# Loading q and k in 128 rows of 18 tokens and turning them with an output stride of 18, in a windowed-attention and expert-attention kernel

## The chip, the cores and the metric

The kernel runs on one core of a Trainium2 chip. Its engines work side by side, each through its own list of instructions in order: TensorE (PE in the profile, with its weight loads as PEld) multiplies matrices out of on-chip memory (SBUF) into the accumulators (PSUM); VectorE (DVE), ScalarE (ACT) and GpSimd (POOL) work on rows of elements; SyncE (SP) issues the transfers (DMAs) between the chip's large memory and SBUF, and ScalarE issues a few of them too. SBUF has 128 partitions, and an instruction of DVE works on all of them at once. The metric is the device time in microseconds of one execution, taken as the median of several runs.

## What is computed

Two steps follow each other. First, attention with a symmetric window of 32 tokens over 8 batches, 8 heads, 576 tokens and 64 elements per head; then, on the outcome, four small attention experts, of which two per token count.

```python
scores = scale * np.matmul(q, k.transpose(0, 1, 3, 2))
mask = np.abs(pos[:, None] - pos[None, :]) <= window
...
attn_out = np.matmul(attn, v).astype(np.float32)
x = attn_out.transpose(0, 2, 1, 3).reshape(B, S, H * D)
logits = x @ w_gate
...
for e in range(E):
    q = x @ wq[e]; k = x @ wk[e]; v = x @ wv[e]
    ...
    ye = a @ v @ wo[e]
```

All inputs and the output are 32-bit floats. q and k have the layout [batch, head, token, element], so that the 64 elements of a token lie together (256 bytes), and the tokens of a head follow each other.

## The kernel before

The product of q and k needs the elements of a head along the partitions, while they arrive with the tokens along the partitions. So each half of the heads of a batch (4 heads, called a group) is loaded with tokens along the partitions and then turned.

**Loading.** `load_qk` (line 268) fills one of three buffers per name, `qn0` to `qn2` and `kn0` to `kn2`, each of 128 partitions x 18 tokens x 64 elements. Head h of the group goes to partitions 32h to 32h+31. In the branch that the kernel before uses throughout, the tokens of a head are cut into 9 blocks of 64, and partition p of the 32 gets tokens 2p and 2p+1 of each block. The source is then made of pieces of two tokens, 512 bytes, and there is one transfer for each head: 32 partitions x 9 pieces, 144 KB. A load of one name for one group of one batch is four such transfers, 576 KB.

**Turning.** `turn` (line 288) makes two instructions of DVE (`STREAM_TRANSPOSE`, 128 x 576), one for each half of the 64 elements. Each turns squares of 32 x 32: element d of 32 tokens becomes partition d's run of 32 elements. Where they are written is set by the access pattern of the output, `T`. There the tokens lie in their natural order, and since the 32 tokens of one square are every second token, a square is written with a stride of two elements (8 bytes). The turned tiles `Tqn` and `Tkn` exist once for each group and half.

**The steps.** The order of all work is written out by hand in `ORDER`: each word is a step, and each engine meets its instructions in the order of the words. A step's name says what it does, with the batch and the group: `lq100` loads q of batch 1, group 0 (the third digit is the part, 0 for the whole), `lk` loads k, `lv` loads a part of v, `tq` and `tk` turn, `sc` multiplies q by k, `ex` takes exponentials (ACT), `mk` multiplies by the window's mask (DVE or POOL), `av` multiplies by v, `un` divides by the sums (DVE), `xt`, `xf` and `xb` turn and copy the outcome for the experts; `pp`, `ps`, `xe`, `se`, `po`, `oe` and the rest are the experts; `st` stores. A letter behind a colon picks a variant: for loads and turns `t` means the same layout through ScalarE's queue, `e` the other branch of the two functions. Batch 0 is loaded in two parts, so that work can begin on the first.

**What holds a load.** `load` (line 184) makes every transfer wait for the last TensorE instruction ahead of it in the list, so a load is not issued before its place in the list is reached. A load into a buffer also waits for the turns that read the buffer's former contents. And transfers of SP and ACT share eight semaphores in turn: each transfer waits until the one eight places ahead of it has landed. SP works through its list in order, so a transfer that waits holds all loads and stores behind it.

Of the kernel before, what the change touches and what calls it, by code (L numbers as in the profile page):

```python
# [24 lines left out]
NOE = 2  # L25

ORDER = """
    s_mask s_pads lq100 lk011:t tk011:t lk001:t tk001:t lq011 lq001 tq011 lq002 lk012:t lk002:t lq012 s_ones
    sc010@02 lv02 lk100 lv01 lv03 s_warm tq001 sc000@46 ex0101@2 ex0001@6 mk0001:g ex0000@4 lv00 s_ident mk0101:g
    tk002:t tk012:t tq002 sc001@24 ex0011@4 mk0011:g mk0000:g tq012 sc011@46 ex0111@6 tq100 tk100 mk0111:g lq110  # L30
    ex0100@0 ex0110@4 vc00:v ex0010@2 mk0010:v lk110 sc101@06 mk0110:v ex1011@6 tq110 ex1010@0 mk1010:v lv04 lw1
    sc100@24 vc01:g av02@0 tk110 lv13 ex1001@4 un02@0 mk0100:g av01@4 un01@4 av00@6 un00@6 lw0 ex1000@2 mk1000:v
    cw0:g av03@2 av04@0 mk1011:g un04@0 sc111@46 un03@2 ex1111@6 cw1:v xt02@0 lw2 cw2:g xt01@2 xf01:v@2 xb01:v
    lq200 lk200 xf02:a@0 xb02:v mk1001:g ex1110@4 xt00@6 xf00:a@6 sc110@04 ga0@6 gt0@6 xb00:a ex1101@4 lv10
    pp001@2 lv12 ex1100@0 mk1100:g lv11 lq210 pp000@0 pe000:v@0 pe001:a@2 pp010@2 pe010:v@2 mk1101:g mk1111:g
    ps003@0 ps000@4 xe003@0 se003 ps002@6 pv00@0 xe000@4 xe002@6 pp011@4 tq200 vc11:g ve00:a@0 pe011:a@4 ps001@6
    xe001@6 tk200 sc200@02 ex2001@2 ps013@4 lv14 xe013@4 mk1110:v lk210 vc10:v lk300 ps010@6 xe010@6 ex2000@0 ge0
    mk2000:g sc201@24 se000 ex2011@4 ex2010@2 se001 ps012@6 tq210 av12@0 mk2011:g un12@0 av10@4 mk2010:g lq300
    pv01@3 xe012@6 ve01:a@3 gm0 lk310 av13@6 av11@0 un10@4 un13@6 un11@0 se012 av14@4 un14@4 tk210 xt11@6 lw3
    xf11:a@6 lv23 xb11:g xt12@0 xf12:v@0 xb12:g xt10@4 lv22 mk2001:g xf10:v@4 xb10:v lv20 ps011@2 xe011@2 sc211@06  # L40
    ex2111@6 ex2110@0 mk2110:v se002 sc210@24 pp110@6 ex2100@2 mk2100:g ex2101@4 lv21 lq310 cw3:g pe110:a@6 gu0
    mk2101:g pp101@2 pe101:a@2 po00@6 pp100@2 tk300 lv24 oe00@6 pp111@4 se011 pt00@6 pe100:v@2 ps102@2 ps103@0
    pe111:a@4 xe102@2 xe103@0 tq300 ga1@7 gt1@7 lq400 ot00:a@6 mk2111:v sc301@24 ex3010@2 ex3011@4 ge1 tk310
    sc300@06 ex3001@6 ps100@2 xe100@2 lk400 tq310 vc21:g se010 av23@4 vc20:g av22@6 un23@4 ex3000@0 pv11@2 un22@6
    ve11:a@2 av20@0 un20@0 av24@7 lk410 un24@7 se013 ps111@4 xe111@4 mk3011:g ps101@2 lv31 xe101@2 av21@0 un21@0
    sc311@46 ex3110@4 tq400 lv30 sc310@02 ex3111@6 xt21@4 lq410 lv44 ex3100@0 mk3100:g ex3101@2 mk3101:g tk400
    xt20@0 xf21:v@4 xt22@2 po01@6 xf20:a@0 xf22:v@2 ps110@4 oe01@6 ps113@0 ga2@2 gt2@2 xb22:v xe113@0 lv33
    mk3110:v xe110@4 gm1 sc401@06 ex4011@6 mk3010:v tk410 lv32 tq410 ex4010@0 xb21:g sc400@24 mk3001:g lv34
    ex4000@2 mk4000:v lv41 ex4001@4 pv10@6 lv42 lq500 pt01@5 ot01:v@5 lv40 ve10:a@6 xb20:g pp200@3 pe200:a@3
    pp210@0 vc30:a pp201@6 gu1 pe210:a@0 pe201:v@6 pv20@4 ps203@6 lk500 ve20:v@4 ps112@0 mk3111:v xe203@6 xe112@0  # L50
    se100 gm2 ps200@2 xe200@2 mk3000:g lv43 vc31:g av31@6 pv21@5 ve21:v@5 un31@6 av30@0 mk4001:g av33@2 un30@0
    un33@2 mk4010:g lv53 se103 av32@4 un32@4 py02@0 ye02:a@0 av34@7 un34@7 lq510 py01@2 xt32@7 ye01:v@2 xf32:a@7
    xb32:v xt31@4 tk500 xf31:a@4 lk510 sc410@06 ex4100@0 sc411@24 ex4111@4 ex4101@6 py00@0 ex4110@2 vc41:g vc40:g
    se101 ye00:a@0 tq500 tq510 lv52 lv50 xt30@4 xf30:v@4 pp211@6 se102 po10@2 oe10@2 pe211:a@6 ps210@6 ps211@4
    ga3@0 gt3@0 lv54 xe210@6 xe211@4 sc500@26 ex5001@6 ex5000@2 se110 sc501@04 ex5011@4 mk4111:v ex5010@0 mk5001:v
    se112 se111 se113 po11@6 oe11@6 lk600 ps201@4 xb30:g mk4100:g lv51 mk4101:g ps212@2 xe201@4 xe212@2 av41@0
    un41@0 av40@6 ps213@4 xe213@4 mk4011:g un40@6 ge3 ps202@0 mk4110:g av44@2 lq600 tk510 se201 xe202@0 un44@2
    xb31:g pp300@4 pt10@0 pp310@6 se211 st02 pt11@1 ot11:a@1 tk600 mk5000:g vc50:g pp301@2 pe301:a@2 xt42@1
    pe310:v@6 pe300:v@4 av42@6 un42@6 av43@2 un43@2 xf42:v@1 st00 ot10:a@0 gm3 py12@0 se203 ye12:a@0 se213
    sc511@46 ex5110@4 ex5111@6 sc510@02 ge2 gu2 st01 lv62 py11@4 ex5100@0 mk5010:g vc51:g ex5101@2 lq700 ye11:a@4  # L60
    pp311@6 se200 pe311:a@6 lk610 xt41@2 gu3 xt40@4 xf40:v@4 lq610 xf41:a@2 pv30@6 mk5111:g ve30:a@6 mk5011:g
    se202 po20@4 xb42:a ps311@2 xe311@2 ps302@0 tq600 ga4@6 oe20@4 gt4@6 xe302@0 sc601@24 mk5100:g mk5110:g
    sc600@06 ex6010@2 ex6011@4 ex6001@6 ps301@2 xe301@2 ex6000@0 mk5101:v se210 se301 av51@4 lv71 xb40:g pv31@6
    ve31:a@6 lk710 gm4 un51@4 av54@7 un54@7 ps310@2 ps300@4 lk700 st12 ps312@0 av52@6 un52@6 xe310@2 av53@2
    xe300@4 un53@2 av50@4 lv61 un50@4 mk6010:v xe312@0 ps313@0 xe313@0 se302 ge4 ps303@2 py10@6 ye10:a@6 xt52@4
    xf52:v@4 xb52:v xe303@2 xt50@0 xf50:a@0 lv73 lv64 xt51@4 xb41:g xf51:a@4 xb51:a lq710 pp410@2 tk610 pe410:a@2
    mk6001:v tq610 pp411@0 pe411:a@0 se212 po21@4 pp401@2 st11 oe21@4 pe401:v@2 lv63 tk700 lv60 pt20@0 mk6000:v
    ot20:a@0 xb50:a se300 se303 po30@6 se312 vc61:g ps411@4 ps412@2 se311 pv40@0 xe411@4 oe30@6 xe412@2 pp400@4
    se412 pe400:v@4 ve40:a@0 tq700 sc610@26 sc611@04 ex6100@2 tk710 ex6101@6 mk6101:v ex6110@0 ps401@2 gu4 xe401@2
    ex6111@4 pp500@6 pp501@0 pe500:a@6 se313 se310 pt21@2 ot21:a@2 po31@4 ps402@6 xe402@6 pe501:v@0 oe31@4 tq710  # L70
# [559 lines left out]
```

## Time and profile before

| what | value |
|---|---|
| median of 3 runs | 264.48 us |
| lowest and highest run | 263.19 and 267.05 us |
| profiled execution, first to last instruction | 262.5 us |
| instructions | 11479 |
| read and written over the span | 152 GB/s |

The profile describes one execution with a span of 262.5 us; the median of the runs is 1.9 us above it. A page of the profile gives the busy time of each engine, then the chain of work that ended last, and then groups of instructions. In a row of a group stand the line, the engine, the operation, the tiles (output<-input), the shape, the count, the busy time in us and the mean of one in ns, and behind the second bar the idle time of the engine just ahead of them and what ended it. In a row of stretches of time stand from and to, the length, the busy time of each engine with the number of instructions in brackets, the granted TensorE clock as a share, the busy share of the 16 DMA engines, and GB/s.

### The profile page before, as it was taken

How to read it: one execution, taken by the hardware profiler on the slowest of the kernel's cores; microseconds unless marked ns; L12 is line 12 of the kernel's file. 1: busy time of each engine (PE TensorE's matmuls, PEld its weight loads, DVE VectorE, ACT ScalarE, POOL GpSimd, SP SyncE). 2: the span in 40 equal slices, each digit the busy share in tenths (PEclk: the TensorE clock that was granted, in tenths of full speed). 3: DMA queues.
4: the chain of work that ended last, by engine and by line, in shares of the span. 5: the costliest groups of instructions: out<-in, count | busy, mean ns of one | idle time of the engine just before them, and what ended most of it. 6: DMA issues, size and time to landing. Idle time of an engine off the chain costs nothing.

```text
span 262.5 us, 11479 instructions
## 1 busy us (share of the span) xinstructions
PE 228.9 (87%) x5013; PEld 183.2 (70%) x5024; DVE 193.2 (74%) x400; ACT 147.0 (56%) x221; POOL 127.2 (48%) x165
## 2 busy tenths in 40 slices
PE   0286999985989999699989999998899989999981
PEld 0165898664768888567878877886688758877650
DVE  2455896759899889998997956986876596667640
ACT  0223416761646557326745677776657657785852
POOL 5019706765686097337967906109734236322400
PEclk9995699999999999999999999999999999999997
DMA  8969989999974598886186798990021520124366
GB/s 166 209 171 180 228 160 211 204 198 226 199 177 138 161 209 176 170 196 162 34 205 201 157 162 159 216 290 15 2 63 42 186 80 2 32 92 157 126 216 208
DMA packets 89362, 40.60 MB, mean 155 GB/s; under 512 B 47072, under 2 KB 84960, under 8 KB 89312
## 3 DMA queue, kind: packets, MB, share of 16 engines
q1 hardware_dynamic: 86752, 38.69, 64.4%
q10 hardware_dynamic: 2560, 1.18, 2.4%
q8 instruction: 39, 0.64, 1.1%
q14 instruction: 11, 0.09, 0.1%
HBM read 30.42 MB, written 9.44 MB: 152 GB/s over the span
## 4 chain that ended last, share of the span: by engine, by line
PE 64%; DVE 16%; DMA 9%; issue 3%; ACT 3%; SPq 2%; POOL 1%; ACTq 0%; DVEq 0%
PE PS L179 57%; PE PS L182 7%; DVE A L340 5%; DMA qn<-in_q_dram 4%; DMA kn<-in_k_dram 4%; SPq L185 2%; ACT A L336 2%; DVE Tkn L298 1%; DVE RG L545 1%; DVE OE L546 1%; DMA out_dram<-Y 1%; DVE XN L368 1%; POOL V L173 1%; DVE Tqn L298 1%; DVE VE L173 1%
## 5 line engine op out<-in xcount | busy, mean ns | idle before, releaser
L179 PE MATMUL PS<-Tqn,Tkn 32*64 32x96 f32 (+5 forms) x2048 | 63.6, 307 | 16.9 <-DVE Tqn L298 11.6
L340 POOL TENSOR_TENSOR A<-A,MASKP 128x576 f32<-128x576 f32 x41 | 59.2, 1458 | 33.1 <-ACT A L336 32.5
L179 PEld LDWEIGHTS PS<-Tqn,Tkn 32*64 32x64 f32 (+1 forms) x2048 | 51.9, 158 | 29.4 <-DVE Tqn L298 12.0
L336 ACT ACTIVATE A<-PS 128x576 f32<-128x576 f32 x64 | 38.9, 650 | 41.0 <-PE PS L179 41.0
L506 ACT ACTIVATE ATE<-PS 128x1024 bf16<-128x1024 f32 x48 | 47.4, 1023 | 8.4 <-PE PS L179 6.8
L511 POOL TENSOR_SCALAR_AFFINE_SELECT ATE<-ATE 128x256 bf16<-128x256 bf16 (+1 forms) x80 | 31.4, 413 | 39.6 <-ACT ATE L506 24.2
L179 PE MATMUL PS<-V,A 128*64 128x65 f32 (+1 forms) x1280 | 39.6, 222 | 3.8 <-DVE XN L368 2.4
L179 PEld LDWEIGHTS PS<-V,A 128*64 128x64 f32 (+1 forms) x1280 | 36.1, 132 | 7.5 <-DVE XN L368 2.9
L173 POOL COPY V<-V 64x2048 f32<-64x2048 f32 (+1 forms) x12 | 21.8, 1820 | 27.3 <-DMA V<-in_v_dram 21.9
L298 DVE STREAM_TRANSPOSE Tkn<-kn 128x576 f32<-128x576 f32 (+2 forms) x36 | 23.2, 686 | 8.4 <-DMA kn<-in_k_dram 7.3
L298 DVE STREAM_TRANSPOSE Tqn<-qn 128x576 f32<-128x576 f32 (+2 forms) x36 | 23.2, 686 | 7.6 <-DMA qn<-in_q_dram 6.6
L340 DVE TENSOR_TENSOR A<-A,MASKP 128x576 f32<-128x576 f32 x23 | 25.3, 1109 | 3.0 <-ACT A L336 3.0
L368 DVE TENSOR_TENSOR XN<-PS,RC 128x512 f32<-128x512 f32 x32 | 22.1, 691 | 1.1
L179 PE MATMUL PS<-WV,XTB 128*128 128x256 bf16 (+1 forms) x192 | 18.8, 255 | 1.1 <-DVE OTT L173 0.8
L179 PE MATMUL PS<-WO,OTT 128*128 128x512 bf16 (+1 forms) x85 | 18.2, 341 | 1.4 <-ACT OTT L171 0.7
L179 PE MATMUL PS<-XTB,WK 128*128 128x288 bf16 x128 | 18.3, 286 | 1.0 <-DVE QKE L173 1.0
L182 PE MATMUL PS<-ident,XN 128*128 128x128 f32 x144 | 18.1, 275 | 1.1 <-DVE XN L373 0.9
L171 ACT COPY Y<-PS 128x1024 f32<-128x1024 f32 (+1 forms) x17 | 13.7, 826 | 9.3 <-PE PS L179 8.3
L179 PE MATMUL PS<-XTB,WQ 128*128 128x288 bf16 x128 | 18.1, 287 | 0.0
L179 PE MATMUL PS<-QKE 64*128 64x64 bf16 (+4 forms) x192 | 16.8, 277 | 1.4 <-DVE QKE L173 1.2
L182 PEld LDWEIGHTS PS<-ident,XN 128*128 128x128 f32 x144 | 15.8, 141 | 3.1 <-DVE XN L373 1.7
L179 PEld LDWEIGHTS <-ATE 128*128 128x128 bf16 x480 | 16.4, 97 | 2.2 <-POOL ATE L511 0.8
(71 smaller groups left out, 279.8 us busy)
## 6 DMA issues: line engine op xcount, KB each, us to landing
V<-in_v_dram SPq DMA_DIRECT2D x32, 256.0 KB, 4.7
out_dram<-Y SPq DMA_DIRECT2D x16, 512.0 KB, 3.8
qn<-in_q_dram SPq DMA_DIRECT2D x56, 144.0 KB, 4.3
kn<-in_k_dram SPq DMA_DIRECT2D x56, 144.0 KB, 4.3
V<-in_v_dram SPq DMA_DIRECT2D x8, 128.0 KB, 4.2
out_dram<-Y SPq DMA_DIRECT2D x16, 64.0 KB, 2.6
kn<-in_k_dram ACTq DMA_DIRECT2D x8, 80.0 KB, 3.5
qn<-in_q_dram SPq DMA_DIRECT2D x8, 80.0 KB, 2.8
```

The source lines that it names most:

```text
L171: nc.scalar.copy(o, i)
L173: eng(c).tensor_copy(o, i)
L179: last_pe[0] = nc.tensor.matmul(*a, **kw)
L182: last_pe[0] = nc.tensor.transpose(*a)
L185: r = q_.dma_start(o, i)
L298: nc.vector.transpose(T[:, 64 * m0:64 * m1].rearrange("q (m p o) -> q m o p", p=32, o=2), n_[:, 2 * m0:2 * m1, 32 * dh:32 * dh + 32].rearr ...
L336: nc.scalar.activation(AT[(2 * b + g) % NAT_][half][p], two(b0)[:, :, 0:HS], EXP, scale=scale_att)
L340: eng(c).tensor_tensor(out=ap, in0=ap, in1=MASK[:, None, HS * half:HS * half + HS].to_broadcast([128, 2, HS]), op=MULT)
L368: nc.vector.tensor_tensor(out=XN[T // 2][:, T % 2, :].rearrange("p (g h d) -> p g h d", g=2, h=4), in0=u[:, :, :, 0:64], in1=rc[:, :, :, N ...
L506: nc.scalar.activation(chunk(A, ch), two(b0), EXP, scale=scale_moe)
L511: nc.gpsimd.affine_select(ap, ap, pattern=[[0, n], [1, w]], compare_op=IS_GE, fill=0.0, base=0, channel_multiplier=-1)
L545: nc.vector.tensor_tensor(out=rg, in0=GG[b % 2][:, 2 * j:2 * j + 2, :], in1=rg, op=MULT)
```

## The change

The word of every load and turn of q and k of batches 1 to 7 in `ORDER` gets the letter `e`. Nothing else differs: the list has the same steps at the same places, the functions are the same, and batch 0 is loaded and turned as before.

```diff
-    s_mask s_pads lq100 lk011:t tk011:t lk001:t tk001:t lq011 lq001 tq011 lq002 lk012:t lk002:t lq012 s_ones
-    sc010@02 lv02 lk100 lv01 lv03 s_warm tq001 sc000@46 ex0101@2 ex0001@6 mk0001:g ex0000@4 lv00 s_ident mk0101:g
+    s_mask s_pads lq100:e lk011:t tk011:t lk001:t tk001:t lq011 lq001 tq011 lq002 lk012:t lk002:t lq012 s_ones
+    sc010@02 lv02 lk100:e lv01 lv03 s_warm tq001 sc000@46 ex0101@2 ex0001@6 mk0001:g ex0000@4 lv00 s_ident mk0101:g
...
-    se412 pe400:v@4 ve40:a@0 tq700 sc610@26 sc611@04 ex6100@2 tk710 ex6101@6 mk6101:v ex6110@0 ps401@2 gu4 xe401@2
+    se412 pe400:v@4 ve40:a@0 tq700:e sc610@26 sc611@04 ex6100@2 tk710:e ex6101@6 mk6101:v ex6110@0 ps401@2 gu4 xe401@2
```

With `e`, `load_qk` takes its first branch: partition p of a head's 32 gets the 18 tokens 18p to 18p+17, which lie together in the source, and the four heads follow each other, so that one transfer fills 128 partitions with one row of 4608 bytes each. `turn` takes its first branch too: the 32 tokens of a square are now 18 tokens apart, and the output is written with a stride of 18 elements (72 bytes) inside a square. The turned tiles hold the same elements at the same places as before.

| per load of q or k, batches 1 to 7 | before | after |
|---|---|---|
| transfers | 4 | 1 |
| partitions x pieces of one transfer | 32 x 9 of 512 bytes | 128 x 1 of 4608 bytes |
| bytes in all | 589,824 | 589,824 |
| turns (DVE) | 2, output stride 8 bytes | 2, output stride 72 bytes |

There are 28 such loads and 56 such turns. Each engine meets its instructions in the same order as before, and on SP 112 of the transfers become 28.

More of the change, by code (lines that the diff above doesn't have):

```diff
@@ L33 @@
-    cw0:g av03@2 av04@0 mk1011:g un04@0 sc111@46 un03@2 ex1111@6 cw1:v xt02@0 lw2 cw2:g xt01@2 xf01:v@2 xb01:v
[L34 to L37, printed above, removed]
@@ new lines @@
+    lq200:e lk200:e xf02:a@0 xb02:v mk1001:g ex1110@4 xt00@6 xf00:a@6 sc110@04 ga0@6 gt0@6 xb00:a ex1101@4 lv10
+    pp001@2 lv12 ex1100@0 mk1100:g lv11 lq210:e pp000@0 pe000:v@0 pe001:a@2 pp010@2 pe010:v@2 mk1101:g mk1111:g
+    ps003@0 ps000@4 xe003@0 se003 ps002@6 pv00@0 xe000@4 xe002@6 pp011@4 tq200:e vc11:g ve00:a@0 pe011:a@4 ps001@6
+    xe001@6 tk200:e sc200@02 ex2001@2 ps013@4 lv14 xe013@4 mk1110:v lk210:e vc10:v lk300:e ps010@6 xe010@6 ex2000@0 ge0
+    mk2000:g sc201@24 se000 ex2011@4 ex2010@2 se001 ps012@6 tq210:e av12@0 mk2011:g un12@0 av10@4 mk2010:g lq300:e
```

53 lines of the change are left out of this document (26 added, 27 removed).

## The prediction

> **What bounds the kernel now.** I read the busy times first, then the chain of work that ended last, then the stretches of time, because a share of the whole span mixes stretches with different limits.
>
> ```profile
> PE 228.9 (87%) x5013; PEld 183.2 (70%) x5024; DVE 193.2 (74%) x400; ACT 147.0 (56%) x221; POOL 127.2 (48%) x165
> ...
> PE 64%; DVE 16%; DMA 9%; issue 3%; ACT 3%; SPq 2%; POOL 1%; ACTq 0%; DVEq 0%
> ```
>
> TensorE sets the end, VectorE (DVE) is second on the chain, and transfers third. The stretches tell where each of them counts:
>
> ```profile
> 0.00:15.00 15.00, 3.23 (x68) 2.61 (x72) 5.62 (x27) 1.65 (x3) 3.87 (x12) 1.00 0.90 183
> 15.00:45.00 30.00, 26.94 (x672) 22.78 (x672) 22.71 (x41) 12.09 (x21) 15.41 (x14) 0.83 0.93 191
> 45.00:65.00 20.00, 15.80 (x361) 12.45 (x358) 14.10 (x22) 9.93 (x17) 14.03 (x14) 1.00 1.15 210
> 65.00:85.00 20.00, 18.74 (x470) 15.11 (x470) 18.49 (x34) 11.63 (x19) 14.10 (x15) 1.00 0.79 176
> 85.00:115.00 30.00, 27.82 (x678) 22.97 (x675) 27.04 (x55) 15.21 (x22) 13.31 (x11) 1.00 0.84 179
> 115.00:135.00 20.00, 18.80 (x497) 14.98 (x497) 17.52 (x29) 12.54 (x20) 16.33 (x19) 1.00 0.52 129
> 135.00:165.00 30.00, 29.76 (x668) 24.36 (x669) 22.75 (x54) 18.39 (x31) 16.49 (x22) 1.00 0.81 177
> 165.00:190.00 25.00, 23.33 (x504) 18.76 (x504) 20.53 (x38) 17.69 (x26) 12.13 (x15) 1.00 0.57 130
> ```
>
> The columns behind the length are PE, PEld, DVE, ACT and POOL, then the granted clock, the DMA share and GB/s. From 65 to 135 us DVE is nearly full: it idles 1.5 us of 20, 3.0 of 30 and 2.5 of 20. From 135 to 165 TensorE alone is full, and DVE has 7.2 us to spare. Up to 65 us the DMA engines are full. Whatever lengthens DVE is paid between 65 and 135, and whatever shortens transfers is won before 65.
>
> **The turns.** Their number does not change, only where they write. Today one whole turn takes
>
> ```profile
> L298 DVE STREAM_TRANSPOSE Tkn<-kn 128x576 f32<-128x576 f32 x28 | 20.0, 754 | 3.8 <-DMA kn<-in_k_dram 2.7 <-PE PS L179 1.1
> L298 DVE STREAM_TRANSPOSE Tqn<-qn 128x576 f32<-128x576 f32 x28 | 19.9, 752 | 2.3 <-DMA qn<-in_q_dram 1.2 <-PE PS L179 1.1
> ```
>
> and all 56 of them, 39.9 us of DVE, become turns with an output stride of 72 bytes. No turn of that kind is in the trace, so I look for pairs of DVE instructions of equal size, one writing its elements side by side, the other apart:
>
> ```profile
> L443 DVE TENSOR_TENSOR G<-NU,su x8: 194/266/1340, 71.8 to 247.0; 128x20 f32<-128x20 f32 x8
> L436 DVE TENSOR_TENSOR PK<-LT,m x8: 178/180/469, 61.9 to 235.3; 128x20 f32<-128x20 f32 x8
> L213 DVE MEMSET V<- x2: 112/112/112, 12.0 to 12.1; 128x64 f32 x2
> L220 DVE MEMSET QKE<- x3: 112/112/112, 1.2 to 1.3; 128x64 uint32 x3
> 1.17 0.26 DVE L220 MEMSET QKE<- 128x64 uint32 x3
> 12.00 0.23 DVE L213 MEMSET V<- 128x64 f32 x2
> ```
>
> The first pair: `G` is written through a rearranged pattern, each element 5 places (20 bytes) from the one before, `PK` side by side; both combine 20 elements with a broadcast. The minima, free of waiting, are 194 and 178 ns: 16 ns for 20 elements, 0.8 ns each. The second pair: line 213 writes the 64 ones of `V` 65 places (260 bytes) apart, line 220 writes runs of 32. Each instruction lasts 112 ns either way, which says no cost. But instructions overlap, and the spacing says otherwise: three of line 220 end 0.26 us after the first begins, so they start (0.26 - 0.112)/2 = 0.074 us apart; two of line 213 take 0.23, so they start 0.118 apart. That is 0.044 us more for 64 elements, 0.69 ns each. Over 576 elements the three readings are 0, 396 and 461 ns per turn; the upper end is a turn that doubles, +753 ns. No reason is seen why a wider stride should be a gain. I take 461 ns, because that row, like a turn, reads SBUF and writes it, while a memset reads nothing; and the spacing agrees. So 56 x 0.461 = 25.8 us more on DVE.
>
> The Trainium skill, page "Advanced Engine Details and Errata", section "Memory Cachelines", speaks against the change: SBUF has lines of 16 bytes, two accesses must fall in one line to cover its latency, and a new line at each access is penalised. At 8 bytes two elements share a line, at 72 none do. It gives no size of the penalty; `G` and the spacing agree with it, the duration of the memset does not. By it the sum would be the one below, and without it that of the first rival.
>
> What DVE pays in each stretch follows from the turns that lie in it:
>
> ```profile
> 15.00:45.00 30.00, 8.64 (x17) 0.83 0.93 191
> 45.00:65.00 20.00, 4.31 (x6) 1.00 1.15 210
> 65.00:85.00 20.00, 7.04 (x10) 1.00 0.79 176
> 85.00:115.00 30.00, 5.50 (x8) 1.00 0.84 179
> 115.00:135.00 20.00, 4.35 (x7) 1.00 0.52 129
> 135.00:165.00 30.00, 4.10 (x6) 1.00 0.81 177
> 165.00:190.00 25.00, 8.60 (x12) 1.00 0.57 130
> ```
>
> A longer DVE eats its own idle time first, but not all of it: part of that idle is time in which TensorE, itself late through DVE, has nothing ready. I let half of it absorb. From 65 to 85: 10 x 0.461 - 0.75 = 3.85. From 85 to 115: 3.7 - 1.5 = 2.2. From 115 to 135: 3.2 - 1.25 = 1.95. From 165 to 190: 5.5 - 2.2 = 3.3. From 135 to 165 the 2.8 us are covered by 7.2 of idle, and from 15 to 45 at most 17 turns, half of them of batch 0 and unchanged, by 7.3. Together 11.3 us; if all idle absorbs 5.5, if none does 17.0.
>
> **The loads.** Each of 28 loads becomes one transfer in place of four. Now:
>
> ```profile
> qn<-in_q_dram SPq DMA_DIRECT2D x56, 144.0 KB, 4.3
> ...
> L185 SPq DMA_DIRECT2D qn<-in_q_dram x72: 311/447/1551, 0.8 to 169.8; - x72
> ...
> SPq L185 <- DMA kn<-in_k_dram: 3.9, 5, 1.7
> ...
> 245.00:262.00 17.00, 11.06 (x140) 7.14 (x140) 6.41 (x17) 9.26 (x12) 2.06 (x6) 0.94 0.59 210
> ```
>
> SP saves 84 issues of 0.447 us, 37.5 us of its time; and since at most eight transfers are under way, a load takes one place of eight, not four. In the first 15 us, where nearly all pieces have 512 bytes, the engines moved 183 GB/s at a share of 0.90, or 203 when full; in the last 17, where stores with rows of 2 KB run, 210 at 0.59, or 356. A load of 589,824 bytes so takes 2.9 us of full engines now and, if long rows of a load run like those of a store, 1.7 after: between 0 and 1.2 us less each.
>
> The Trainium skill, page "DMA: Bandwidth & Descriptors", section "Rules for kernel authors", asks for 128 partitions and large single transfers. By it alone the change would be won; the rows say where that can count.
>
> At most places it can't: a load is held until its place in the list, and its turn has slack. It counts at the start, where the chain is four waits for transfers in a row, and from 49 to 57 us, where DVE stands still for loads:
>
> ```profile
> 1.26 3.93 DMA kn<-in_k_dram
> 5.57 2.95 DMA kn<-in_k_dram
> 8.54 2.75 DMA kn<-in_k_dram
> 11.30 2.85 DMA qn<-in_q_dram
> ...
> 49.91 1.44 DVE L298 STREAM_TRANSPOSE Tkn<-kn 128x576 f32<-128x576 f32 x2 [1.19 <-DMA kn<-in_k_dram]
> 54.26 1.22 DVE L173 COPY V<-V 64x1536 f32<-64x1536 f32 x1 [2.27 <-DMA V<-in_v_dram]
> 56.71 1.44 DVE L298 STREAM_TRANSPOSE Tqn<-qn 128x576 f32<-128x576 f32 x2 [1.23 <-DMA qn<-in_q_dram]
> ```
>
> The start: `lq100` is the very first load on SP and shares the engines with batch 0. It gives back up to 1.2 us; I take 1.0. From 45 to 65 the three stalls are 4.7 us, while TensorE idles 4.2. Loads issued earlier take the stalls away; six longer turns put 2.8 back. I take 1.5 us won. What is late next there is DVE itself.
>
> **The sum** against the profiled execution: 262.5 + 11.3 - 1.0 - 1.5 = 271.3 us, and with the 1.9 us by which the median of the runs lies above that span, 273.2. With all idle absorbed 267.4, with none 278.9.
>
> **The rivals.** *The wide stride costs nothing* (the memset's 112 ns are the truth). Then only the loads count: 1.0 at the start and, of the 4.2 us that TensorE idles from 45 to 65, about 3; the rest waits for other things. 262.5 - 4.0 + 1.9 = 260.4 us, between 257.5 and 263. It decides while a turn gains less than about 240 ns: at that price the same rule gives 1.65 + 0.4 + 0.45 + 0.7 = 3.2 us of loss, as much as the loads then win (1.0 and 2.2). Against it stand `G` and the spacing, for it that turns drain at their own pace.
>
> *A turn doubles*, +753 ns. By the same rule: 6.75 + 4.5 + 4.0 + 6.8 = 22.1 us, the stretch from 45 to 65 wins nothing, the start 1.0: 262.5 + 21.1 + 1.9 = 285.5 us. For it speaks only that no row has a stride inside squares of 32.
>
> *The start gets worse*: the one transfer of `lq100` holds its place of the eight until all 576 KB have landed, and the transfer of k that comes eight later waits for it, ahead of batch 0's first scores. If the chain's second link, 2.95 us, starts 1.2 later, the 1.0 won is 1.2 lost: 275.4.
>
> That the change does not do what it says is excluded for the instructions, which are as described in the compiled program; whether one transfer of 128 rows keeps all 16 engines busy no row shows.
>
> **How the numbers follow.** Costly stride as summed 0.62, costless 0.25, doubling 0.08, worse start 0.05. The forecast is the first, 273. Its own range is 266 to 280. For 8 in 10 the range also has to reach most of the costless case: 259 to 281; outside stay the doubling, the lower third of the costless case and a little of the first, about 0.19. Two per cent, about what separates a change of this kernel from none, is 5.3 us: faster means under 259.2, slower over 269.8. Faster: a third of the costless case, 0.08. Slower: 0.7 of the first and both last, 0.56. Within: the rest, 0.36.
>
> **What would show it.** The row of the turns: near 1210 ns (right), near 750 (first rival), near 1500 (second). DVE's busy time: 219 us. The stretch that holds batch 1 to 4's turns after 65 us: DVE with hardly any idle, TensorE waiting for turned tiles. The first scores: at 13.8 us in place of 14.80. The three stalls from 49 to 57 gone. The prediction is wrong if turns are slow and yet hidden (the time within 265), or if loads win over 6 us.

## The result: 281.0 us, slower than forecast, and the profile after

| | before | changed |
|---|---|---|
| median of the runs | 265.43 us | 281.0 us |
| lowest and highest run | 263.19 and 267.05 | 279.47 and 284.89 |
| ratio, with its interval | | 1.0652 [1.0577, 1.0727] |
| ratio in a second comparison, 5 rounds | | 1.0643 [1.0592, 1.0694] |

The forecast was 273 us with a range up to 281. The direction was right and the loss was nearly twice the size: 15.6 us where 8.7 had been summed. Ratios here and below compare the fast executions of both kernels alone (an execution more than 1.5 per cent above the fastest of its kernel counts as slow), so they are not the quotients of the medians, which go by all. All rows of the changed kernel below are from the profile of the second comparison (span 281.0 us, 18.5 above that of before; the medians of that comparison, 283.53 and 266.12 us, are 17.4 apart). First its page:

```profile
PE 233.5 (83%) x5024; PEld 185.0 (66%) x5024; DVE 219.3 (78%) x400; ACT 147.2 (52%) x221; POOL 125.6 (45%) x165
...
PE 53%; DVE 32%; DMA 6%; issue 5%; ACT 2%; ACTq 0%; DVEq 0%
...
L294 DVE STREAM_TRANSPOSE Tqn<-qn 128x576 f32<-128x576 f32 x28 | 32.3, 1237 | 3.0 <-PE PS L179 3.0
L294 DVE STREAM_TRANSPOSE Tkn<-kn 128x576 f32<-128x576 f32 x28 | 32.5, 1240 | 0.5 <-PE PS L179 0.5
L340 DVE TENSOR_TENSOR A<-A,MASKP 128x576 f32<-128x576 f32 x23 | 31.9, 1397 | 2.6 <-ACT A L336 2.6
```

A turn takes 1237 to 1240 ns where it took 752 to 754: 485 more, and 461 had been forecast. DVE's busy time is 219.3 us, as forecast to the microsecond (217.0 and 217.5 in two other executions), and its share of the chain doubled from 16 to 32 per cent. But the last row is a surprise, and makes the agreement partly luck: DVE's 23 products with the window's mask, which the change does not touch, took 25.3 us before,

```profile
L340 DVE TENSOR_TENSOR A<-A,MASKP 128x576 f32<-128x576 f32 x23 | 25.3, 1109 | 3.0 <-ACT A L336 3.0
```

and take 31.9 now; some other rows of DVE got shorter. The stretches of the prediction again, with the columns as there:

```profile
15.00:45.00 30.00, 23.30 (x658) 19.58 (x647) 26.19 (x37) 10.30 (x18) 14.64 (x13) 0.94 0.71 171
45.00:65.00 20.00, 16.81 (x367) 13.11 (x364) 17.18 (x22) 11.89 (x20) 14.27 (x14) 1.00 0.77 241
65.00:85.00 20.00, 17.03 (x389) 13.35 (x396) 18.72 (x32) 9.06 (x15) 12.23 (x14) 1.00 0.62 157
85.00:115.00 30.00, 24.76 (x616) 20.43 (x600) 27.20 (x40) 15.31 (x24) 14.64 (x12) 1.00 0.57 152
115.00:135.00 20.00, 18.68 (x402) 14.65 (x405) 18.43 (x36) 9.12 (x15) 6.93 (x11) 0.91 0.54 143
135.00:165.00 30.00, 27.08 (x640) 21.94 (x630) 27.10 (x46) 16.17 (x27) 21.76 (x22) 1.00 0.52 161
190.00:215.00 25.00, 20.74 (x507) 17.05 (x497) 19.67 (x32) 12.54 (x21) 11.11 (x16) 0.86 0.08 18
```

The DMA engines are no longer full ahead of 65 us (0.71 and 0.77 of their time, before 0.93 and 1.15), and the granted clock is below 1.00 in two stretches behind 100 us where before it was not. Where the 18.5 us arise is read from TensorE's list, which is the same in both kernels: the start of the same product in the two traces, taken next to the forecast's boundaries.

| stretch (us, before) | delay of TensorE at its end | gained in it | forecast |
|---|---|---|---|
| 0 to first score product | 0.9 | 0.9 | -1.0 |
| to 45 | 2.8 | 1.9 | 0 |
| 45 to 65 | 1.9 | -0.9 | -1.5 |
| 65 to 85 | 4.2 | 2.3 | 3.85 |
| 85 to 115 | 9.2 | 5.0 | 2.2 |
| 115 to 135 | 10.4 | 1.2 | 1.95 |
| 135 to 165 | 12.2 | 1.8 | 0 |
| 165 to 190 | 18.05 | 5.85 | 3.3 |
| 190 to the end | 18.5 | 0.45 | 0 |

Two stretches stand out, 85 to 115 and 165 to 190, and with them the start and the stretch to 45. The last is worse than the table says, for there the two traces also differ in the clock: before has it at 0.50 from 21.0 to 31.2 us, this execution of the changed kernel only from 31.3 to 34.7. So TensorE was 0.8 us early at 25 us and 2.7 early at 31.6, and lost 5.5 from there to 45. The timeline of the changed kernel (start, length, engine, line, operation, and in brackets the idle time ahead of it and what ended it) shows what TensorE waited for there:

```profile
12.54 6.16 PE L179 MATMUL PS<-Tqn,Tkn 32*128 32x192 f32 x132 [12.54 <-DVE Tqn L298]
...
31.80 4.83 PE L179 MATMUL PS<-V,A 128*64 128x65 f32 x112 [1.16 <-DVE A L340]
37.61 0.67 PE L179 MATMUL PS<-V,A 128*32 128x65 f32 x32 [0.99 <-DVE XN L368]
...
65.17 0.67 PE L179 MATMUL PS<-V,A 128*32 128x65 f32 x32 [1.93 <-DVE XN L368]
...
96.67 0.70 PE L179 MATMUL PS<-Tqn,Tkn 32*64 32x160 f32 x26 [1.10 <-issue]
...
115.22 1.03 PE L179 MATMUL PS<-WV,XTB 128*128 128x256 bf16 x8 [3.66 <-DVE OTT L173]
...
193.42 1.41 POOL L340 TENSOR_TENSOR A<-A,MASKP 128x576 f32<-128x576 f32 x1
193.94 4.60 DVE L340 TENSOR_TENSOR A<-A,MASKP 128x576 f32<-128x576 f32 x1
195.17 2.75 POOL L340 TENSOR_TENSOR A<-A,MASKP 128x576 f32<-128x576 f32 x2
199.19 0.75 DVE L173 CAST QKE<-PS 128x576 bf16<-128x576 f32 x1
199.99 5.75 PE L179 MATMUL PS<-Tqn,Tkn 32*128 32x128 f32 x128 [4.01 <-DVE QKE L173]
```

In before these two waits are 0.82 us and none, and the product that DVE starts at 193.94 reads

```profile
179.62 0.72 DVE L340 TENSOR_TENSOR A<-A,MASKP 128x576 f32<-128x576 f32 x1
```

The wait of 3.66 us at 115 is in part as forecast: two turns (109.73 to 114.21) stand ahead of the copy of `OTT` in DVE's list, 2 x 2 x 0.485 = 1.9 us longer together. Ahead of them, a product with the mask at 107.35 takes 2.45 us where it took 0.75, beside a copy of POOL. The wait at 200 is not as forecast. One product of DVE lasts 4.60 us in place of 0.72; it ends at 198.54, which is 0.62 us behind the end of POOL's three products (195.17 + 2.75 = 197.92). It did not work for 4.60 us, it stood until POOL was through and then took its own time. And the 128 score products behind the wait last 5.75 us. Three windows of the same trace, laid on the places where the clock falls, show one reason:

```profile
31.30:34.70 3.40, 2.90 (x54) 2.91 (x56) 3.40 (x5) 0.00 (x0) 0.00 (x0) 0.50 0.45 85
116.70:120.10 3.40, 3.40 (x54) 2.72 (x56) 2.29 (x7) 2.22 (x3) 0.00 (x0) 0.50 0.61 174
198.60:205.40 6.80, 5.41 (x122) 4.52 (x124) 5.20 (x11) 1.19 (x2) 0.00 (x0) 0.50 0.01 2
```

At each of them the granted clock is 0.50, for 3.4 or 6.8 us, behind or within a wait of TensorE. So there are at least three things to separate: DVE's lost time itself, what waits do to the clock, and what the shift does to DVE and POOL, which meet at other times.

### The profile page after: what moved, and what is told of

Same layout as the page of the kernel before. It is cut to its first block, busy times and chain, and to the rows that moved or that the text cites. A ratio compares the mean times of both kernels' runs of the same rounds, so it can differ in the third digit from the quotient of the medians.

```text
span 283.1 us, 11352 instructions
## 1 busy us (share of the span) xinstructions
PE 237.3 (84%) x5013; PEld 189.1 (67%) x5024; DVE 217.5 (77%) x400; ACT 147.3 (52%) x221; POOL 125.7 (44%) x165
## 4 chain that ended last, share of the span: by engine, by line
PE 53%; DVE 31%; DMA 6%; issue 6%; ACT 2%; ACTq 0%; DVEq 0%
PE PS L179 47%; DVE A L340 7%; PE PS L182 7%; DVE Tqn L294 5%; DVE Tkn L294 5%; DMA kn<-in_k_dram 4%; DVE XN L368 2%; DVE OE L546 2%; DVE QKE L173 2%; ACT A L336 1%; DMA qn<-in_q_dram 1%; DMA out_dram<-Y 1%; DVE RG L545 1%; DVE L L424 1%; DVE XTB L173 1%
## 5 line engine op out<-in xcount | busy, mean ns | idle before, releaser
L179 PE MATMUL PS<-Tqn,Tkn 32*64 32x160 f32 (+5 forms) x2048 | 65.6, 310 | 23.0 <-DVE Tqn L298 12.3
L179 PEld LDWEIGHTS PS<-Tqn,Tkn 32*64 32x64 f32 (+1 forms) x2048 | 52.8, 159 | 36.4 <-DVE Tqn L298 12.3
L179 PE MATMUL PS<-V,A 128*64 128x65 f32 (+1 forms) x1280 | 41.6, 228 | 7.9 <-DVE XN L368 4.3
L179 PEld LDWEIGHTS PS<-V,A 128*64 128x64 f32 (+1 forms) x1280 | 37.7, 137 | 12.3 <-DVE XN L368 4.8
L294 DVE STREAM_TRANSPOSE Tqn<-qn 128x576 f32<-128x576 f32 x28 | 32.3, 1236 | 2.8 <-PE PS L179 2.8
L294 DVE STREAM_TRANSPOSE Tkn<-kn 128x576 f32<-128x576 f32 x28 | 32.5, 1239 | 0.5 <-PE PS L179 0.5
L173 POOL COPY V<-V 64x2048 f32<-64x2048 f32 (+1 forms) x12 | 21.4, 1783 | 22.8 <-DMA V<-in_v_dram 12.2
L340 DVE TENSOR_TENSOR A<-A,MASKP 128x576 f32<-128x576 f32 x23 | 28.7, 1258 | 2.6 <-ACT A L336 2.6
L182 PE MATMUL PS<-ident,XN 128*128 128x128 f32 x144 | 20.6, 302 | 0.4 <-DVE XN L373 0.2
L182 PEld LDWEIGHTS PS<-ident,XN 128*128 128x128 f32 x144 | 18.4, 157 | 2.5 <-DVE XN L373 0.9
L171 ACT COPY Y<-PS 128x1024 f32<-128x1024 f32 (+1 forms) x17 | 13.6, 826 | 11.9 <-PE PS L179 8.0
L179 PEld LDWEIGHTS <-XTB 128*128 128x128 bf16 (+1 forms) x192 | 14.9, 106 | 6.6 <-issue 4.7
```

Source lines behind the costliest of these rows:

```text
L171: nc.scalar.copy(o, i)
L173: eng(c).tensor_copy(o, i)
L179: last_pe[0] = nc.tensor.matmul(*a, **kw)
L182: last_pe[0] = nc.tensor.transpose(*a)
L294: nc.vector.transpose(T[:, :].rearrange("q (p o) -> q o p", o=18)[:, o0:o1], n_[:, o0:o1, 32 * dh:32 * dh + 32])
L340: eng(c).tensor_tensor(out=ap, in0=ap, in1=MASK[:, None, HS * half:HS * half + HS].to_broadcast([128, 2, HS]), op=MULT)
```

## The experiments

### The change once more

> The changed kernel once more, for a profile beside the others. Theory A (turns cost 485 ns more each, and the stalls they make let the granted TensorE clock fall to half, which lengthens matmuls in turn): 278 to 283 us, turns at 1.24 us each, TensorE busy 7 to 9 us more than before for the same matmuls, and some 15 us more at half clock. Theory B (the larger transfers cost a good part of the loss, by holding their places among the eight in flight): the same time, but the engines wait for transfers of q and k by 4 us or more over the parts behind the start.

Measured: 283.04 us (277.96 to 283.66). And with five rounds:

> The changed kernel again, beside the next two on one chip. Both theories: 1.055 to 1.07 of the kernel before.

Measured: 283.53 us, ratio 1.0643 [1.0592, 1.0694], the profile shown above. In the trace of the first of these two runs the clock was at half for 24 us ahead of 250 us, in the second for 13.7, and yet the spans are 281.5 and 281.0 us: where it falls, and how often, differs between executions of one kernel, and the sum of the time at half does not tell how long one takes. What stays in both is the waits ahead of the products at 115 and 200 us (2.23 and 3.98; 3.66 and 4.01). The first is 1.4 us shorter where the product with the mask ahead of the turns takes 0.75 us (in the other, 2.45). Theory B's waits are not there: DVE waits for q and k at the start alone (8.7 us, batch 0), and no longer behind it.

### The two halves apart

One kernel has the old loads and the new turns, the other the new loads and the old turns. In both the tokens then stand in another order, with the same instructions and sizes, so that only their times can be used.

```diff
-    lq200:e lk200:e ... tq200:e ... tk200:e
+    lq200 lk200 ... tq200:e ... tk200:e        (turns_only, all of batches 1 to 7)
+    lq200:e lk200:e ... tq200 ... tk200        (loads_only)
```

> The loads are those of the kernel before (four transfers of 512-byte pieces), the turns write with the stride of 18; the tokens so come out in another order, with the same instructions and sizes. Theory A: all of the loss and the loads' gain gone as well, 280 to 286 us. Theory B: the turns alone give what was summed for them, 262.5 + 11.3 and 1.9 on top, some 275 us or less.

Measured: 278.93 us, ratio 1.0507 [1.0392, 1.0621], between the two theories. Again with five rounds:

> The wide turns with the old loads (tokens in another order), once more. If the loads add a loss of their own when turns are slow: 1.045 to 1.055 of the kernel before, at least 0.8 per cent below the changed kernel. If they add nothing: within 0.6 per cent of the changed kernel.

Measured: 1.0479 [1.0405, 1.0553].

> The loads are single transfers of 128 rows, the turns write with the stride of 2 as before; again the tokens come out in another order. Theory A: faster than before, 258 to 262 us, with the three stalls of VectorE between 49 and 57 us gone. Theory B: slower than before, 267 us or more.

Measured: 265.91 us, ratio 1.0018 [0.9969, 1.0067]: neither theory. In its trace TensorE is 0.8 us late at the first product and 1.3 late at 45 us, then 1.3 early at 65, and it stays 1.1 to 1.4 early from there on. So the loads win 2.6 us between 45 and 65, where the forecast had 1.5, and lose 1.3 ahead of it, where the forecast had a gain of 1.0. The whole loss is the turns', and the loads add to it only beside slow turns: 1.0643 against 1.0479.

### The price of a stride

A kernel of DVE instructions alone, each three times on 576 elements per partition; the rest of the computation is left out.

```python
for _ in range(3): nc.vector.transpose(wide(k), P1)   # L79 to L85: output stride k = 1, 2, 3, 4, 5, 8, 18
for _ in range(3): nc.vector.transpose(W1[:, 0:576].rearrange("q (p o) -> q o p", o=18), P1)   # L90
for _ in range(3): nc.vector.tensor_tensor(out=flat(k), in0=W2[:, 0:576], in1=W2[:, 576:1152], op=MULT)   # L91 to L97
for _ in range(3): nc.vector.tensor_tensor(out=W2[:, 0:576], in0=flat(k), in1=W2[:, 576:1152], op=MULT)   # L98 to L104
```

> Leaves out the whole computation: only instructions of VectorE on 128 x 576 32-bit elements, three of each kind, turns and products of two tiles, with an output stride of 1, 2, 3, 4, 5, 8 and 18 elements, and products with such a stride on an input. If what counts is how many elements share 16 bytes: turns near 735 ns at 1 and 2, between at 3, near 1235 from 4 on, all alike, and the same steps for products. If it is a collision of certain strides: 8 and 18 differ from 4 and 5 and from each other. If it is the turn's own drain: products keep their time at all strides.

Measured, in groups by line (the last number ahead of the second bar is the mean in ns):

```profile
L90 DVE STREAM_TRANSPOSE W<-src 128x576 f32<-128x576 f32 x3 | 3.8, 1258 | 0.1
L85 DVE STREAM_TRANSPOSE W<-src 128x576 f32<-128x576 f32 x3 | 3.8, 1257 | 0.1
L97 DVE TENSOR_TENSOR W<-W 128x576 f32<-128x576 f32 x3 | 3.7, 1235 | 0.1
L104 DVE TENSOR_TENSOR W<-W,W 128x576 f32<-128x576 f32 x3 | 3.7, 1229 | 0.1
...
L82 DVE STREAM_TRANSPOSE W<-src 128x576 f32<-128x576 f32 x3 | 3.6, 1199 | 0.1
...
L81 DVE STREAM_TRANSPOSE W<-src 128x576 f32<-128x576 f32 x3 | 2.8, 938 | 0.1
...
L80 DVE STREAM_TRANSPOSE W<-src 128x576 f32<-128x576 f32 x3 | 2.3, 779 | 0.1
...
L79 DVE STREAM_TRANSPOSE W<-src 128x576 f32<-128x576 f32 x3 | 2.3, 759 | 0.1
```

A turn takes 759, 779, 938 and 1199 ns at strides of 4, 8, 12 and 16 bytes, and 1257 at 72. The step is at 16 bytes: up to 8 a stride costs nearly nothing, at 12 some 160 to 180 ns, from 16 on 420 to 500 ns on 576 elements, 0.72 to 0.87 ns each. A product pays the same whether it writes (1235) or reads (1229) with the stride. This is the rule of the Trainium skill that the prediction weighed ("Advanced Engine Details and Errata", "Memory Cachelines": lines of 16 bytes, two accesses in one line, a penalty else), and this trace agrees with it and gives the size that the page does not have.

### DVE's lost time, or something else that the stride disturbs

Old loads, old turns, and behind each whole turn a second one of 416 elements into a tile that nobody reads:

```diff
                 nc.vector.transpose(T[:, 64 * m0:64 * m1].rearrange(...), n_[...].rearrange(...))
+                if b > 0:
+                    nc.vector.transpose(PAD[:, :].rearrange("q (o p) -> q o p", p=32), n_[:, 0:13, 32 * dh:32 * dh + 32])
```

> The kernel before, with an extra turn of 13 squares (416 elements, about 490 ns) into a spare tile behind each of the 56 whole turns; all writes side by side or 8 bytes apart. Theory A (the loss is the time that VectorE loses, wherever it comes from): slower than before by as much as the wide turns alone, 1.04 to 1.06. Rival (wide writes also hinder other engines' access to SBUF): clearly less, under 1.03.

Measured: 280.76 us, ratio 1.0462 [1.04, 1.0525], as with the wide turns alone (1.0479). An added turn lasts 569 ns, so that DVE's list got 31.9 us longer, by wide turns 27.2. Filling it with work of no use, at no wide stride, costs much the same: the stride acts through DVE's time.

### The first load

```diff
-    s_mask s_pads lq100:e ... tq100:e
+    s_mask s_pads lq100 ... tq100
```

> The changed kernel with the very first load (q of batch 1, group 0) and its turn as in the kernel before. If that single transfer of 576 KB, ahead of batch 0's, is what delays the start: the first products begin at 11.6 to 11.9 us in place of 12.3 to 12.6, and the time falls by about 1 us. If not: the first products begin as late as with the change.

Measured: 281.34 us, ratio 1.0603 [1.0552, 1.0655]; the first score product starts at 11.61 us, before at 11.64, in the change at 12.54. The ratio is not clear of the change's 1.0643, but the trace shows that the loss at the start is that one transfer's. In the change's chain, k's first transfer takes longer to land, and the second starts 1.1 us later than in before (5.57):

```profile
1.25 5.39 DMA kn<-in_k_dram
6.66 2.97 DMA kn<-in_k_dram
```

### Steps moved away from the waits

In the change, and as a control in the kernel before, the steps that stood on DVE ahead of three awaited results are put behind them:

```diff
-    pv01@3 xe012@6 ve01:a@3 gm0 lk310:e ... un14@4 tk210:e
+    pv01@3 xe012@6 ve01:a@3 lk310:e ... un14@4 gm0 tk210:e
-    mk3010:v tk410:e lv32 tq410:e ex4010@0 ... pe201:v@6 pv20@4
+    mk3010:v lv32 ex4010@0 ... pe201:v@6 tk410:e tq410:e pv20@4
-    ex6101@6 mk6101:v ex6110@0 ... pe501:v@0 oe31@4
+    ex6101@6 ex6110@0 ... pe501:v@0 mk6101:v oe31@4
```

> The changed kernel with four VectorE steps at later places of the list: gm0 behind un14, tk410 and tq410 behind pe201, the mask product mk6101 behind pe501. Theory A (a slow turn costs where it, or a step it pushes into GpSimd's work, stands ahead of something TensorE needs): the waits ahead of av14, pv20 and sc701 (1.8, 2.2 and 4.0 us) shrink to under 1 us each and the time falls by 5 to 9 us. Rival (VectorE is full there, so another wait takes their place): less than 2 us.

Measured: 283.84 us, ratio 1.0665 [1.0602, 1.0728].

> The kernel before with the same four steps moved. Theory A: the wait ahead of av14 (2.4 us) shrinks, the rest had little wait: 1 to 3 us faster than before. Rival: no difference, or slower.

Measured: 265.48 us, ratio 0.9988 [0.995, 1.0026]. Nothing was won. Two turns behind the copy of `OTT` made the next awaited result late instead, by 3.6 us, and behind the moved mask product this came up in the timeline of the changed kernel with moved steps:

```profile
200.45 3.71 DVE L440 TENSOR_TENSOR NU<-EX,PK 128x20 f32<-128x20 f32 x1
...
201.35 2.76 POOL L340 TENSOR_TENSOR A<-A,MASKP 128x576 f32<-128x576 f32 x2
...
205.52 4.85 PE L179 MATMUL PS<-Tqn,Tkn 32*128 32x128 f32 x124 [3.04 <-DVE QKE L173]
```

A product of 20 elements, 0.38 us at its place in before, lasts 3.71 us and ends at 204.16, just as POOL's last product does (204.11). The long mask product of the change was no property of that product: another DVE instruction with two SBUF inputs stands there in its place.

Nor is it a matter of one instruction. In the kernel with the old loads and wide turns (five rounds) the same place reads

```profile
195.03 1.84 DVE L340 TENSOR_TENSOR A<-A,MASKP 128x576 f32<-128x576 f32 x1
196.80 1.74 DVE L440 TENSOR_TENSOR NU<-EX,PK 128x20 f32<-128x20 f32 x1
...
200.62 4.87 PE L179 MATMUL PS<-Tqn,Tkn 32*128 32x128 f32 x128 [3.55 <-DVE QKE L173]
```

The mask product is short there, others stand instead, and TensorE waits nearly as long. From the start of the mask product to the copy that TensorE waits for, DVE takes 1.66 us before, 5.25 in the change, 4.79 here and 4.02 with padded turns. So the time of the mask products alone, 31.9 us for 25.3, is no measure of what the meeting with POOL costs.

### Products of no use against TensorE's waits

To see what the waits do to the clock, unneeded products of TensorE (of the unit matrix with itself, into a free piece of an accumulator) are put ahead of four of the products that wait:

```diff
+    def fl(c, n, b0):
+        for _ in range(n):
+            mm(PS[:, b0, 448:512], ident, ident[:, 0:64], start=True, stop=True, skip_group_check=True)
...
-    cw0:g av03@2 ...  av13@6 av11@0 ...  pe201:v@6 pv20@4 ...  ot21:a@2 po31@4
+    cw0:g fl8@2 av03@2 ...  av13@6 fl7@0 av11@0 ...  pe201:v@6 fl8@4 pv20@4 ...  ot21:a@2 fl14@4 po31@4
```

> The changed kernel with 128 extra products of the unit matrix in four places, just ahead of the TensorE work at whose end it stands still for VectorE (before av03 and av11 of the first two batches, pv20 and po31); their results are not read. Theory A1 (the fall of the clock to half is a cost of its own): the granted clock stays whole behind those four places and the time falls by 3 to 7 us below the changed kernel, though TensorE has more to do. Theory A2 (VectorE's lateness alone binds, TensorE's clock only follows): the time stays within 1.5 us of the changed kernel, or grows by the extra work.

Measured with 128 of them (28, 24, 28, 48): 293.74 us, ratio 1.108 [1.1024, 1.1135]. Each took some 230 ns, twice the estimate, so that 29.5 us were added: far more than the waits, and the time says little. Behind the start the clock was at half for 3.4 us only.

> As the kernel with 128 extra products, with 37 of them: at 230 ns each as measured there, 8.5 us of extra work, about as long as the waits ahead of av04, av14, pv20 and sc701 (10.4 us). Theory A1 (the fall of the clock costs by itself): no half clock behind those places, and 3 to 6 us less than the changed kernel. Theory A2 (VectorE binds anyway): within 1.5 us of the changed kernel, though the clock stays whole.

Measured with 37 (the numbers in the diff; 8.5 us): 276.44 us, ratio 1.0396 [1.034, 1.0452], 7 us less than the change, with more work for TensorE. The same 37 in the kernel with the old loads:

> The loads of the kernel before, wide turns (so the tokens stand in another order), and the 37 added unit products of filled_less at the same four places. A1, the clock's fall is a cost of its own wherever waits of 2 us appear: the half clock behind them goes, and the time is 273 to 276 us against 278.9 and 281.7 of the same kernel without the products, a ratio near 1.035. A2, the gain of filled_less came from an order of loads and turns that happened to fit: the time is 280 to 287 us, as long as without the products or longer by up to their 8.5 us.

Measured: 276.43 us, ratio 1.0417 [1.0366, 1.0467], between what A1 and A2 had for it. Without the products it was 1.0479 [1.0405, 1.0553]; the intervals overlap, so a gain is not shown here. Its clock from 32 us up to 0.7 us ahead of its end:

```profile
32.00:140.00 108.00, 99.03 (x2342) 81.04 (x2327) 101.02 (x158) 53.73 (x84) 57.99 (x58) 1.00 0.79 163
140.00:274.00 134.00, 124.66 (x2412) 97.81 (x2406) 96.69 (x202) 86.15 (x126) 53.27 (x85) 1.00 0.48 128
```

It did not fall there (from 20 to 31 us the weight loads of the score products take 212 ns, which is the half pace, as in before from 21 to 31). In the two traces of the same kernel without the products it was at half for 13.7 us in that time. Behind 32 us, slow turns are seen here without a fall of the clock: TensorE is 9.45 us late at 165 and 12.1 at 190 and 240, near the 11.3 of the forecast's sum for the turns, but with up to 8.5 us of products in it. In the change, the time at half clock is the same in sum with the products (13.6 us, 21.8 to 32.0 and 131.0 to 134.4) and without them (13.7); what differs is where it lies. The place at 200 us in the change with 37 products:

```profile
190.39 0.75 DVE L340 TENSOR_TENSOR A<-A,MASKP 128x576 f32<-128x576 f32 x1
...
191.01 3.34 PE L179 MATMUL PS<-ident 128*128 128x64 f32 x28
...
195.51 3.46 PE L179 MATMUL PS<-Tqn,Tkn 32*128 32x128 f32 x128
```

The mask product takes 0.75 us again, since it comes 0.06 us ahead of POOL's first product (190.45), which this time is the one to stand, 1.94 us for 1.41; TensorE waits for nothing there; and the 128 score products take 3.46 us at full clock in place of 5.75. All of DVE's mask products take 24.4 us in this kernel (31.9 in the change). So A1 stands for that place: the 128 products last 2.3 us longer at half clock. It is not shown for the 7 us: the products also shift waits and the meeting with POOL away, and this experiment does not split them.

The same idea at the start of the kernel before, where the clock is at half from 21.0 to 31.2 us:

```diff
-    ... sc001@24 ... sc011@46 ... sc101@06
+    ... fs4@2 sc001@24 ... fs3@4 sc011@46 ... fs5@0 sc101@06
```

> The kernel before with 12 small unneeded products of TensorE (4, 3 and 5, some 0.1 us each) ahead of the score products that wait between 18 and 26 us, just ahead of the stretch of 10 us at half clock. A1: the stretch at half clock gets shorter by 3.4 us or more, and the time falls by 1 to 3 us (ratio 0.989 to 0.996), or by less as far as transfers set the pace there. A2, the half clock there comes from the products themselves, which keep TensorE busy for short times only: no change, 0.997 to 1.005.

Measured: 267.72 us, ratio 1.0027 [0.9981, 1.0073]. Over the window from 15 to 45 us the profile gives the clock as 1.00 (0.83 before), as if the stretch at half were gone. But its record of the clock begins only at 35.2 us there, and the weight loads of the score products say otherwise (first this kernel at 29.6 to 35.4 us, then before at 25.9 to 31.2 at a granted clock of 0.50, then the change with 37 products at 195.5 to 199 at 1.00):

```profile
L179 PEld LDWEIGHTS PS<-Tqn,Tkn 32*64 32x64 f32 x96 | 2.7, 210 | 0.7 <-issue 0.7
```

```profile
L179 PEld LDWEIGHTS PS<-Tqn,Tkn 32*64 32x64 f32 x89 | 2.4, 210 | 0.7 <-issue 0.7
```

```profile
L179 PEld LDWEIGHTS PS<-Tqn,Tkn 32*64 32x64 f32 x96 | 1.7, 130 | 0.3 <-issue 0.2
```

They run at the half pace up to 35 us, longer than in before. So the products did not take the half pace away, they drew it out: the score products of batch 1 came 3.7 us late (29.66 for 25.92), of which 1.9 were left at 63 us. The experiment doesn't test A1. No version here is clearly faster than the kernel before.

### Which loads cost more beside slow turns

Wide turns throughout, single transfers for batches 1 to 3 or for batches 4 to 7.

```diff
+    lq100:e ... lk310:e lq400 ... lk710          (loads_early)
+    lq100 ... lk310 lq400:e ... lk710:e          (loads_late)
```

> Wide turns throughout, single transfers for batches 1 to 3 alone (12 loads; the tokens of batches 4 to 7 stand in another order). C1, the extra 1.6 per cent comes from the early loads, which change the order in which transfers land while the DMA engines are full: a ratio of 1.060 to 1.066. C2, it comes from the late ones: 1.045 to 1.051.

Measured: 279.45 us, ratio 1.0515 [1.0457, 1.0574].

> Wide turns throughout, single transfers for batches 4 to 7 alone (16 loads; the tokens of batches 1 to 3 stand in another order). C1: a ratio of 1.045 to 1.051, as with the old loads. C2: 1.060 to 1.066. If both this and the early one lie near 1.055, the cost is spread over all loads.

Measured: 281.48 us, ratio 1.0615 [1.056, 1.067]: the late ones, C2, though the two intervals overlap a little. The waits view of the kernel with late single transfers and of that with none (engine, line, what it waited for, us in total, times, longest):

```profile
PE PS L179 <- issue: 2.7, 3, 1.4
```

```profile
PE PS L179 <- issue: 0.2, 1, 0.2
```

TensorE there stands 2.7 us for nothing that the profile shows, in the change itself 1.8 (among it the 1.10 at 96 us), and with the old loads 0.2 or 0.8. And DVE's mask products take 29.4 us, against 25.3 and 26.5 in the two runs with the old loads. The second has to do with POOL: with the old loads its copy of `V` at 188 to 191 us waits for the transfer (11 us idle, ended by `DMA V<-in_v_dram`), with late single transfers it waits for none and comes earlier against DVE's product, and so do POOL's products behind it. But at that place this costs little: TensorE waits 4.02 us there with late single transfers, 3.55 and 3.36 in the two traces with the old loads. Laid beside the slower of these, the trace with late single transfers loses 1.4 us between 85 and 95 us, where TensorE's queue stands, and 0.5 at 200. The queue is the larger part, as far as two traces tell; what holds it is not shown.

### POOL's products taken away from the worst place

```diff
-    vc60:g mk6100:g av61@3 ... xe500@6 mk6111:g
+    vc60:g mk6100:v av61@3 ... xe500@6 mk6111:v
```

> The change with two of POOL's mask products of batch 6 given to DVE, some 5 us behind the place at which DVE's product took 4.6 us in the change while POOL ran three products. D1, DVE's two-input product stands until POOL's products end, and this is what the wait of 4.0 us and the half clock at 196 to 205 us come from: one product of POOL is left there, DVE's takes at most 2.2 us, TensorE's wait falls from 4.0 to 1.5 us or less, and the kernel gets 2.5 to 6 us faster, 277.5 to 281 us, a ratio of 1.045 to 1.055. D2, DVE's debt from its slow turns sets that place, the long product only shows it: another DVE instruction takes the wait, and with 1.4 us more on DVE the time stays, a ratio of 1.062 or more.

Measured: 282.53 us, ratio 1.0608 [1.0565, 1.0651].

> The same edit on the kernel before, where no such collision lies: D1 and D2 alike 0.997 to 1.005, so that a gain in the change is not one of the edit by itself.

Measured: 266.48 us, ratio 1.0053 [1.0029, 1.0077]. In the changed kernel with this edit:

```profile
195.83 1.38 DVE L340 TENSOR_TENSOR A<-A,MASKP 128x576 f32<-128x576 f32 x1
...
196.54 1.92 POOL L340 TENSOR_TENSOR A<-A,MASKP 128x576 f32<-128x576 f32 x1
197.13 1.37 DVE L440 TENSOR_TENSOR NU<-EX,PK 128x20 f32<-128x20 f32 x1
...
199.87 4.94 PE L179 MATMUL PS<-Tqn,Tkn 32*128 32x128 f32 x128 [2.01 <-DVE QKE L173]
```

DVE's product falls from 4.60 to 1.38 us, and TensorE's wait from 4.01 to 2.01: D1 in the trace. D1 missed in the time, and so did its half for the control: the edit costs 0.5 per cent in the kernel before, since TensorE then waits for the two products on DVE (1.2 and 1.5 us, in both kernels), and this takes most of what the place gives back. Against its control the changed kernel with the edit stands at 1.0608 / 1.0053 = 1.0552, the change without it at 1.0643; without the control, 1.0608 and 1.0643 are not clear of each other. That the meeting with POOL costs some 2 us here is what the rows show; that it would be won as time has not been shown.

## Why the prediction was wrong, and where it was right

*The turns*: right. 461 ns were taken from a pair of 20-element products, 485 were measured, so the first rival (a costless stride) and the second (a doubling, +753) both fell. That DVE's busy time came out as forecast (219 and 219.3) is partly luck: its waits beside POOL were not in the sum.

*How much of that TensorE pays*: this is where the prediction failed, and first in the step that from 15 to 45 and from 135 to 165 the longer turns "are covered" by idle time, 7.3 and 7.2 us. Both were put at 0; TensorE lost 1.9 and 1.8 there. The first is more where the clock up to 31 us is as in before: in the five-round trace with wide turns and old loads the delay grows from 0.0 us at 25 to 5.3 at 45, a stretch at half clock from 38.0 included. Idle time of DVE covers a longer turn only if it lies ahead of the next result that TensorE waits for; at 36 us the turn of `Tkn` stands directly ahead of the division whose outcome is the next operand. In the change, four turns of `Tkn` stand between 145.2 and 150.3 us ahead of a copy of `QKE`, 4 x 0.485 = 1.9 us longer, and TensorE then waits for that copy for 1.46 us, which it does not in before. The rule that half of the idle time absorbs was no better elsewhere: it gave too much from 65 to 85 (3.85 for 2.3) and from 115 to 135 (1.95 for 1.2), and too little in the two stretches below.

*The start*: -1.0 became +0.9. The third rival had the place and nearly the size: the one long transfer, issued first, delays the chain of batch 0, whose second link starts 1.1 us later (1.2 in the rival); it was given a chance of 0.05. The time of 14.80 us that the prediction takes for the first scores is that of a later product on the chain, which came 0.7 late; the first one starts at 11.64.

*The loads from 45 to 65*: right. The three stalls of DVE are gone, and the loads alone win 2.6 us there (1.5 forecast); in the change 0.9 are left after the longer turns.

*What the sum did not hold*: that the change moves DVE's work against POOL's, that TensorE can run at half clock behind a wait, and that its own queue can stand. The stretches 85 to 115 and 165 to 190 gave 10.8 us where 5.5 had been summed. In the first, 2.8 us come with the wait at 115 (two longer turns, and a mask product that stands 1.7 longer beside POOL) and 1.4 with the wait at 96 for which the profile shows no cause. In the second, 4.1 come with the wait at 200, where DVE takes 5.25 us for what took 1.66, and the products behind it last 2.3 longer than at full clock. The meeting with POOL does not belong to the stride: with padded turns, and even with the new loads alone, DVE takes 4.02 and 3.88 us at that place; it comes with a shift of DVE's work, whatever makes it.

Of the 9.7 us by which the sum of 8.8 fell short of the 18.5 between the two spans, these two stretches are 5.3, the start 1.9 and the two "covered" stretches 3.7, with the others taking off 1.2.

Open is how much of the time the clock costs in all, since runs with the same waits and nearly the same span had 14 and 24 us at half, and what makes TensorE's own queue stand where single transfers come late.

## What to carry to other kernels

Before a layout is chosen for the sake of a transfer, look at the stride that it leaves to the engine behind it: at 16 bytes or more, each 32-bit element of DVE's work cost 0.72 to 0.87 ns more here, whether it was read or written, and a full DVE pays most of it in the end time. Do not call a longer instruction covered because its engine idles somewhere in the stretch: look whether the idle time lies ahead of the next awaited result. A sum of engine times can fall short of a slowdown: ask what the shift makes collide (here DVE's two-input products with POOL's work). A saving on an engine or queue that did not set the end, like 84 fewer issues on SP here, was worth nothing by itself. And when a clock is read from a record, set the durations of like instructions beside it.

## What the hardware showed that was not expected

*DVE stands still for POOL.* A product of DVE with two SBUF inputs that comes beside POOL's products can last until these end and then its own time: 4.60 us for 0.72, 3.71 for a product of 20 elements. The Trainium skill, "SBUF — State Buffer", section "SBUF: two separate sides", has this as a pair of ports that the two engines take in turn as an exclusive lock; the rows agree, POOL's product that stood in its turn included (1.94 us for 1.41, where DVE's came 0.06 us earlier). One thing more: in these two cases DVE did not get its turn between three products of POOL in a row, with an instruction of another kind (a select) between the first and the second; in the trace with wide turns and old loads above it did, behind the first.

*The clock falls behind short waits.* Stretches at 0.50 last 3.4, 6.8 or 10.2 us (the last one of a trace apart). The Trainium skill's page "TensorE: Matmul & The Clock Gate", section "HAM oscillation — how this bites in real kernels", warns of idle gaps of more than some 3.4 us. The rows agree with the unit of 3.4 us, and with the falls at the waits of 3.66 and 4.01 us; but in the three-round trace with wide turns and old loads the clock fell at 38.0 and 68.7 us, each under 1.5 us behind a wait of 2.20 and 1.72 us, and in the change itself a wait of 1.93 at 63 us was followed by none. No length was found here from which it falls.

*The record of the clock can begin late.* In the trace of before with 12 small products it begins at 35.2 us, and the profile gives 1.00 ahead of it, while weight loads take 210 ns there that take 130 at full clock. Three more traces here begin theirs at 32 to 33 us.

*A duration can hide a price.* The memset that writes 64 elements 260 bytes apart lasts 112 ns like the one that writes runs, in the profile of before; only the spacing of two such instructions showed the 0.7 ns per element, near what the turns and products with a wide stride showed above.
